# A Fourier mixer and a gated unit on one core: relayout of the first batch on VectorE, six chunks a batch on GpSimd, and new list offsets

## The chip, the cores and the metric

The kernel runs on one core of one Trainium2 chip. The metric is the device time of one execution in microseconds (us). The kernel before took 314.53 us in the median of three runs (318.61, 312.99, 314.53). The profiled execution, from which all rows in this document come, is a separate one and took 310.74 us, of which 309.0 us lie between its first and its last instruction.

## The reference

For each of 8 batches, `x` of 3200 positions and 256 channels goes through a real Fourier transform along the positions, is multiplied by a complex filter, and is transformed back. The result feeds a gated unit with a causal convolution over five positions for each channel:

```python
X = np.fft.rfft(x, axis=1)
Y = X * (filt_r + 1j * filt_i)[None, :, :]
y = np.fft.irfft(Y, n=3200, axis=1)
gate_pre[:, s] = sum(conv_w[k] * y[:, s + k - 4] for k in range(5))
out = ((1 / (1 + np.exp(-gate_pre))) * (y @ w_val)) @ w_out
```

## The kernel before

The transform of length 3200 is done as 100 x 32. All work is cut into tasks, each with a name of a stage, a batch and a number. The stages of batch `b`, in order of dependence:

- `li`, `lx`: GpSimd issues five loads for the batch (four of 96 partitions, one with the last four rows of all), which cast `x` to bf16 on the way into `xt`. The tile pool holds two batches.
- `s1` (L539): eight tasks of four matmuls with the table `cf_t`, each over a block of 32 channels and all four loads. `so` copies each result out of PSUM, `t` (L560) turns it on VectorE in 32 x 32 blocks into `tt`.
- `s2` (L570): seven chunks of frequencies (six of two, the last of one) with the table `w_t`.
- `xs`, `z` (L591): the product with the filter `f_t`. In batches 1 to 7 the chunks 1 to 5 are copied out of PSUM (`xs`) and multiplied on GpSimd; chunks 0 and 6 are multiplied by VectorE straight from PSUM. In batch 0 all seven are copied out and multiplied on VectorE.
- `ia` (L604): the first inverse step; `ue` copies out. Then the data changes layout through DRAM: `wr` (L624) writes a scratch tensor `escr`, and `lv` (L634, L635) reads it back as `vt`, once all seven writes of the batch have landed.
- `ib` (L644): the second inverse step, with the table `ci_t`; `ye` copies it out into `y_t`, one of two halves of the time signal's storage.
- `cv` (L665), `ga` (L676): the convolution with diagonal tiles `dg_t` in 32 x 32 blocks of TensorE, and the sigmoid on ScalarE. `cv` of a batch needs all eight `ye` of it. `vl` (L685) and `gv` (L696) make the gated value on TensorE and VectorE, `op` (L705) the output product, `oe` its copy out of PSUM, `store` the write.

Tasks of the kind "copy out of PSUM" (`so`, `xs`, `ue`, `ye`, `oe`) run on ScalarE or on VectorE; both helpers stand in one function, so that all of them appear as L264 (ScalarE) or L266 (VectorE). PSUM has four slots of 1024 words.

The order on every engine is fixed when the kernel is built. The class `Plan` holds a cost for each task, and at each step issues the ready task with the smallest rank. A rank is

```python
par["PERIOD"] * b + par["OFF"][s] + par["STEP"][s] * k + more
```

for stage `s`, batch `b` and number `k`; `more` comes from `HEAD` and differs from zero in batches 0, 1 and 7. `STAY` holds TensorE in one kind of matmul, `HOLD` and `UNTIL` keep copies from VectorE while ScalarE is about to be free. Costs and ranks only set the order of issue; on the chip each engine runs its list in order and waits where its operands are not there.

The filter is loaded by 24 transfers from GpSimd's queue (`fi`, L325 and L329), in two cuts: frequencies 0 to 5 (chunks 0 to 2) and 6 to 12 (chunks 3 to 6). Each cut is then doubled onto other partitions: the first by four transfers from SyncE's queue (`di`, L338), the second by four copies on VectorE (`dx`, L340). The first `z` needs the whole first cut. Transfers from GpSimd's queue run in the order of issue and share the 16 DMA engines with those of SyncE's queue.

Of the kernel before, what the change touches and what calls it, by code (L numbers as in the profile page):

```python
# [16 lines left out]
L = 100  # L17
R = 32
# [13 lines left out]
ZG = (1, 2, 3, 4, 5)  # L32
# [8 lines left out]
    PERIOD=69.33,  # L41
    STAY=17.41, HOLD=0.011, UNTIL=595.53,
    OFF=dict(ci=893.25, cv=136.43, dg=133.01, f=-99.31, ia=98.64, ib=140.46, lv=651.32, lx=112.25, op=334.8,
             pads=6.11, s1=79.04, s2=-92.81, tab=-546.84, vl=-14.07, wtn=485.78, wts=853.38, z=-353.3,
             zp=126.74),
    STEP=dict(ci=131.829, cv=29.199, dg=2.091, f=48.78, ia=21.353, ib=22.278, lv=131.77, lx=8.372, op=9.386,
             pads=12.629, s1=3.933, s2=18.8, tab=72.012, vl=60.741, wtn=92.585, wts=60.233, z=99.415,
             zp=53.742),
    HEAD={
        0: dict(ci=-528.2, cv=-3.9, dg=102.12, f=-304.44, ia=230.55, ib=-168.14, lv=-173.59, lx=172.89,  # L50
             op=-8.32, pads=454.98, s1=-170.57, s2=49.09, tab=-917.46, vl=2.17, wtn=-336.16, wts=-367.93,
             z=92.17, zp=106.55),
        1: dict(ci=183.19, cv=-50.24, dg=104.68, f=49.05, ia=-320.73, ib=-66.17, lv=65.54, lx=-361.7,
             op=0.84, pads=-248.75, s1=-427.17, s2=-23.57, tab=-126.37, vl=10.42, wtn=18.08, wts=-351.07,
             z=137.9, zp=68.79),
        2: dict(ci=79.61, cv=-396.79, dg=204.22, f=-51.32, ia=-236.72, ib=-480.77, lv=65.54, lx=294.66,
             op=-0.81, pads=-238.81, s1=18.19, s2=-77.31, tab=8.17, vl=496.8, wtn=143.78, wts=-454.11,
             z=324.38, zp=166.29),
# [152 lines left out]
def kernel(  # L211
# [20 lines left out]
    ci_t = cpool.tile([128, L], FP16, name="ci_t")  # L232
    w_t = cpool.tile([128, NS, 64], FP16, name="w_t")
# [7 lines left out]
    wn_t, wq_t = (y_t[0][...].rearrange("p h n -> p (h n)")[:, o:o + 2 * D]  # L241
                  .rearrange("p (h e) -> p h e", h=2) for o in (2 * NS * 64, 2 * NS * 64 + 2 * D))
# [10 lines left out]
    gpool = ctx.enter_context(tc.tile_pool(name="gate", bufs=NGB))  # L253
    opool = ctx.enter_context(tc.tile_pool(name="ost", bufs=NOB))

    V = nc.vector
    st, g = {}, {}

# [9 lines left out]
    def small(shape, dtype, name):  # L268

        words = math.prod(shape[1:]) * (1 if dtype == FP16 else 2) // 2  # L270
        o = g["small"] = g.get("small", NS * 64) + words
        assert o <= H + N, o
# [32 lines left out]
    def load_x(b, j):  # L305
        w = R // NX
        if j == 0:
            st["X", b] = xpool.tile([128, NX, XROW], BF16, name="xt")
# [53 lines left out]
    def pool_setup():  # L362
# [3 lines left out]
        for j in range(NX + 1):  # L366
            load_x(0, j)
# [38 lines left out]
    def w_dve():  # L406
# [28 lines left out]
        g["sg"] = sg  # L435
# [48 lines left out]

    def ci_dve():
# [11 lines left out]
        for o, t in zip((vm, vt, vh, vc), fields):  # L497
            V.tensor_copy(o[...], t[...])
        kv, ph, wt, mt = col("kv"), col("ph"), col("wt"), col("mt")
        V.tensor_scalar(ph[...], vc[...], 25.0, 25.0, op0=ALU.mult, op1=ALU.add)  # L500
        V.scalar_tensor_tensor(kv[...], vt[...], 13.0, vm[...], op0=ALU.mult, op1=ALU.add)
        V.scalar_tensor_tensor(kv[...], vh[...], 26.0, kv[...], op0=ALU.mult, op1=ALU.add)
        ix = small([128, L], FP32, name="ix")
        ts(vc[...], vc[...], 1.0, ALU.add)
        V.tensor_scalar(ix[...], g["af"][...], kv[:, 0:1], ph[:, 0:1], op0=ALU.mult,
                        op1=ALU.add)
        ts(mt[...], kv[...], 0.0, ALU.is_equal)
        ts(ix[...], ix[...], 0.01, ALU.mult)
        V.scalar_tensor_tensor(mt[...], kv[...], 50.0, mt[...], op0=ALU.is_equal, op1=ALU.add)
        V.tensor_scalar(wt[...], kv[...], 50.5, 2.0, op0=ALU.is_lt, op1=ALU.mult)  # L510
        g["fx"] = frac(ix, "x", [128, L])
        V.tensor_tensor(mt[...], mt[...], vc[...], op=ALU.mult)
        V.tensor_tensor(wt[...], wt[...], mt[...], op=ALU.subtract)
        ts(wt[...], wt[...], 1.0 / L, ALU.mult)
        g["wt"] = wt

    def ci_act():
        g["sx"] = small([128, L], FP32, name="sx")
        sine(g["sx"][...], g["fx"][...])

    def ci_mul():
        ts(ci_t[...], g["sx"][...], g["wt"][:, 0:1], ALU.mult)
# [23 lines left out]

    def so(b, q, e):
# [5 lines left out]
    def turn(b, q):  # L553
        if q == 0:
# [3 lines left out]
                    for v in (st.pop(("SO", b, q))[...],  # L558
# [37 lines left out]
    def inva(b, u):  # L596
# [3 lines left out]
        for a in range(nm):  # L600
            for w, tab in enumerate((a_t, b_t)):
                for t, h in ((0, 0), (1, 1), (0, 1), (1, 0)):
                    rows = slice(64 * t, 64 * t + 64)
                    nc.tensor.matmul(  # L604
                        ps[64 * h:64 * h + 64, 512 * t + D * a:512 * t + D * a + D],
# [5 lines left out]
    def ue(b, u, e):  # L611
        nm = UCH[u][1]
        ps = st.pop(("ia", b, u))
        t = st["U", b, u] = upool.tile([128, 2, 2, D], BF16, name="u")
# [3 lines left out]
    def wr(b, u):  # L618
        if ("E", b) not in st:
# [7 lines left out]
            in_=t[:, 0:nm].rearrange("p m t d -> p (m t) d"))  # L627

# [43 lines left out]
    def gate(b, j):  # L672
        n = 128 * BLK[j][1]
        ps = st.pop(("cv", b, j))
        t = st["G", b, j] = gpool.tile([128, 2, 512], BF16, name="gt")
# [15 lines left out]
    def gv(b, j):  # L691
        n = 128 * BLK[j][1]
        gt = st.pop(("G", b, j))
        ps = st.pop(("vl", b, j))
        t = st["GV", b, j] = gpool.tile([128, 2, 512], BF16, name="gv")
# [3 lines left out]
    def outp(b, j):  # L699
        nm = BLK[j][1]  # L700
        t = st.pop(("GV", b, j))[:, :, 0:128 * nm].rearrange("p h (n a) -> p h a n", a=nm)
# [7 lines left out]
    def oe(b, j, e):  # L709
        nm = BLK[j][1]  # L710
        ps = st.pop(("op", b, j))
        o = st["O", b, j] = opool.tile([128, 4 * D], FP32, name="o")
        copy(e, o[:, 0:nm * D], ps[:, 0:nm * D])

    def store(b, j):
        m0, nm = BLK[j]
        o = st.pop(("O", b, j))
# [5 lines left out]
    plan = Plan(dict(ring=43, ps=NPS, xt=NXT, so=NSO, t=2, xs=NXS, z=NZ, u=NU, e=2, v=NVB, y=2, g=NGB, gv=NGB,  # L723
# [16 lines left out]
    for b in range(B):  # L740
        for j in range(NX + 1):
# [6 lines left out]
            else:  # L748
                add(f"li0,{j}", {"none": 0.0}, 0, [], None, take=ring, lag=3.2 + 0.55 * j)
            add(f"lx{b},{j}", {"DQ0": 1.97 if j < NX else 0.4}, r, [f"li{b},{j}"], None,  # L750
                lag=SBUF0, packet=0.324, give=ring)
        for q in range(NQ):
            r = rank("s1", b, q)
            add(f"s1{b},{q}", {"PE": 0.456}, r, [f"lx{b},{j}" for j in range(NX + 1)]
# [7 lines left out]
        for u, (m0, nm) in enumerate(UCH):  # L762
            r = rank("s2", b, u)
            cut = [n for n, c in enumerate(FCUT) if m0 < c[1]][0]
            pool = b > 0 and u in ZG
# [5 lines left out]
            if near:  # L771
# [10 lines left out]
                lambda e, b=b, u=u: inva(b, u), take=("ps", "u"), give=("z",), mode=1)  # L782
            add(f"ue{b},{u}", two(512 * nm), r, [f"ia{b},{u}"],
                lambda e, b=b, u=u: ue(b, u, e), give=("ps",), slot=(f"ia{b},{u}", 0))
            add(f"wi{b},{u}", {"SP": 0.37}, r, [f"ue{b},{u}"] + ([f"wi{b},{u - 1}"] if u else []),
# [3 lines left out]
        for i, (r0, nr) in enumerate(ICH):  # L789
            r = rank("lv", b, i)  # L790
            add(f"vi{b},{i}", {"SP": 0.75}, r, [f"wd{b},{u}" for u in range(NU_)],
# [6 lines left out]
                lambda e, b=b, i=i: ib(b, i), take=("ps",) + (("y",) if i == 0 else ()),  # L798
                give=("v",) + (("e",) if i == NI - 1 else ()), mode=0)
            add(f"ye{b},{i}", two(200 * nr), r, [f"ib{b},{i}", "pads"] + (  # L800
                [f"te{len(TCH) - 1},1", "cim", "dg"] if b == 1 and i == 0 else
# [121 lines left out]
```

## Time and profile before

| What | Value |
|---|---|
| Median of three runs | 314.53 us |
| Profiled execution: time, span | 310.74 us, 309.0 us |
| Busy share of the span: TensorE, VectorE, ScalarE, GpSimd | 83%, 81%, 74%, 58% |
| Mean granted TensorE clock | 0.974 |
| DMA | 70.35 MB, mean 228 GB/s |
| Chain that ended last | TensorE 50%, DMA 20%, VectorE 16%, GpSimd 5% |

The profiled time is 1.74 us longer than its span, which lies before the first and behind the last instruction. The shares are means over stages that differ: at the start TensorE has little to do, later almost no gap. A busy matmul need not run at full clock. Rows of a group of instructions give line, engine, operation, tiles, shapes and count, then busy time and the mean ns of one, then the idle time ahead of them. Rows of windows give the stretch, its length, and each engine's busy time with its count of instructions, then the granted clock, the DMA share and GB/s.

### The profile page before, as it was taken

The page shows a single profiled execution, that of the slowest core. Times are in us where ns is not written, and L with a number is a line of the kernel's source. Part 1 is how long each engine was busy: PE and PEld are TensorE (multiplying, and loading weights), DVE is VectorE, ACT ScalarE, POOL GpSimd, SP SyncE. Part 2 cuts the span into 40 slices and gives each one's busy share as a digit, 9 for nine tenths or more (in the row PEclk, how much of TensorE's full clock was granted, in tenths as well). Part 3 has the DMA queues.
Part 4 walks back from the last instruction along what each step waited for, and adds up shares of the span by engine and source line. Part 5 has one row for each costly group of instructions (what it writes and reads, how often), then busy time and mean ns, then how long its engine had stood idle before and what let it go on. Part 6 is the DMA issues. An engine that isn't in the chain of part 4 may idle for free.

```text
span 309.0 us, 11427 instructions
## 1 busy us (share of the span) xinstructions
PE 258.0 (83%) x4932; PEld 174.3 (56%) x4932; DVE 250.5 (81%) x304; ACT 228.8 (74%) x260; POOL 179.3 (58%) x117
## 2 busy tenths in 40 slices
PE   0292499948978999987997999899999999999993
PEld 0151244435645765664765667665776765767662
DVE  6976599984997989997997999797998895686763
ACT  2382488965997889778888778777988886767653
POOL 8394402499899889869922995079803992000000
PEclk9999999965999999999999999999999999999998
DMA  7999995989749999799889988963697687584665
GB/s 109 185 128 228 206 201 134 201 208 237 178 126 199 311 255 303 239 211 311 208 270 216 346 286 221 318 223 131 212 330 260 220 283 237 210 282 161 240 258 223
DMA packets 53154, 70.35 MB, mean 228 GB/s; under 512 B 6256, under 2 KB 35568, under 8 KB 53104
## 3 DMA queue, kind: packets, MB, share of 16 engines
q1 hardware_dynamic: 46032, 54.55, 52.5%
q0 software_dynamic: 7072, 15.08, 29.5%
q8 instruction: 39, 0.64, 0.8%
q14 instruction: 11, 0.09, 0.1%
HBM read 43.78 MB, written 39.85 MB: 271 GB/s over the span
## 4 chain that ended last, share of the span: by engine, by line
PE 50%; DMA 20%; DVE 16%; POOL 5%; issue 4%; ACT 3%; DVEq 0%; SPq 0%; ACTq 0%; POOLq 0%
PE ps L705 11%; PE ps L665 10%; PE ps L685 10%; DMA xt<-in_x_dram 8%; PE ps L539 6%; PE ps L644 5%; PE ps L604 5%; DMA vt<-escr 5%; DVE z L591 4%; DMA out_dram<-o 4%; DMA escr<-u 3%; DVE y L266 2%; PE ps L570 2%; DVE xs L266 2%; DVE tt L560 2%
## 5 line engine op out<-in xcount | busy, mean ns | idle before, releaser
L591 POOL TENSOR_TENSOR z<-xs,f_t 128x2048 bf16<-128x2048 bf16 x35 | 142.2, 4079 | 45.7 <-ACT xs L264 33.5
L696 DVE TENSOR_TENSOR gv<-ps,gt 128x1024 bf16<-128x1024 f32 (+1 forms) x56 | 61.3, 1105 | 14.8 <-PE ps L685 11.1
L676 ACT ACTIVATE gt<-ps 128x1024 bf16<-128x1024 f32 (+1 forms) x56 | 49.7, 930 | 14.7 <-PE ps L665 13.6
L264 ACT ACTIVATE so<-ps 128x1024 bf16<-128x1024 f32 x51 | 51.6, 1024 | 9.7 <-PE ps L539 8.1
L685 PE MATMUL ps<-y,wv_t 128*128 128x512 bf16 (+1 forms) x224 | 52.1, 357 | 2.2 <-issue 0.8
L705 PE MATMUL ps<-wo_t,gv 128*128 128x256 bf16 x400 | 51.9, 273 | 1.1 <-DVE gv L696 0.6
L539 PE MATMUL ps<-xt,cf_t 100*128 100x256 bf16 x256 | 47.6, 326 | 3.9 <-DMA f_t<-in_filt_i_dram 1.3
L705 PEld LDWEIGHTS <-gv 128*128 128x128 bf16 x400 | 41.3, 110 | 6.3 <-issue 2.3
L560 DVE STREAM_TRANSPOSE tt<-so 128x512 f32<-128x512 f32 x64 | 44.0, 700 | 0.6 <-ACT so L264 0.3
L665 PE MATMUL ps<-y,dg_t 32*32 32x512 bf16 (+1 forms) x2240 | 40.9, 355 | 3.2 <-DVE y L266 2.0
L264 ACT ACTIVATE u<-ps 128x1024 bf16<-128x1024 f32 (+1 forms) x39 | 37.6, 968 | 7.5 <-PE ps L604 7.1
L264 ACT ACTIVATE o<-ps 128x1024 f32<-128x1024 f32 (+1 forms) x34 | 31.7, 943 | 10.5 <-PE ps L705 9.4
L644 PE MATMUL ps<-ci_t,vt 104*128 104x100 f16 x512 | 34.4, 212 | 6.0 <-DMA vt<-escr 4.3
L604 PE MATMUL ps<-z,a_t 64*64 64x256 bf16 x416 | 30.2, 304 | 9.9 <-DVE z L591 8.2
L264 ACT ACTIVATE xs<-ps 128x1024 bf16<-128x1024 f32 (+1 forms) x28 | 28.1, 1008 | 13.6 <-DVE z L591 7.5
L644 PEld LDWEIGHTS <-vt 104*128 104x128 bf16 x512 | 28.2, 100 | 16.6 <-DMA vt<-escr 7.2
L264 ACT ACTIVATE y<-ps 128x800 bf16<-128x800 f32 x35 | 29.3, 839 | 10.7 <-PE ps L644 9.7
L539 PEld LDWEIGHTS <-cf_t 100*128 100x128 f16 x256 | 26.5, 112 | 18.8 <-issue 9.4
L266 DVE CAST y<-ps 128x800 bf16<-128x800 f32 x29 | 28.4, 987 | 8.4 <-PE ps L644 6.2
L665 PEld LDWEIGHTS <-dg_t 32*32 32x32 bf16 x2240 | 25.8, 88 | 15.3 <-issue 8.7
L570 PE MATMUL ps<-tt,w_t 64*64 64x256 bf16 x416 | 25.0, 312 | 8.1 <-DVE tt L560 5.7
L685 PEld LDWEIGHTS <-wv_t 128*128 128x128 bf16 x224 | 19.6, 97 | 19.7 <-issue 7.5
(71 smaller groups left out, 249.1 us busy)
## 6 DMA issues: line engine op xcount, KB each, us to landing
out_dram<-o SPq DMA_DIRECT2D x32, 512.0 KB
xt<-in_x_dram POOLq DMA_DIRECT2D x32, 384.0 KB, 7.4
escr<-u SPq DMA_DIRECT2D x48, 256.0 KB
vt<-escr SPq DMA_DIRECT2D x64, 192.0 KB
out_dram<-o SPq DMA_DIRECT2D x24, 384.0 KB
escr<-u SPq DMA_DIRECT2D x8, 128.0 KB
vt<-escr SPq DMA_DIRECT2D x64, 16.0 KB
f_t<-f_t SPq DMA_DIRECT2D x4, 192.0 KB
```

What stands on the lines that cost most here:

```text
L264: nc.scalar.activation(dst, src, AF.Copy, **kw)
L266: V.tensor_copy(dst, src)
L539: nc.tensor.matmul(ps[:, w * CQ * j:w * CQ * j + w * CQ], lhsT=cf_t[0:L].rearrange("p h c i -> p (h c i)"), rhs=st["X", b][0:L, j, 0:w * D ...
L560: V.transpose(dst, src)
L591: eng.tensor_tensor(z[:, :, :, 0:nm * D], src.unsqueeze(1).to_broadcast((128, 2, 2, nm * D)), f_t[:, :, :, m0:m0 + nm, :].rearrange("p w h ...
L604: nc.tensor.matmul(ps[64 * h:64 * h + 64, 512 * t + D * a:512 * t + D * a + D], lhsT=tab[rows, h, m0 + a, :], rhs=z[rows, w, h, D * a:D * ...
L644: nc.tensor.matmul(ps[:, o:o + L], lhsT=v[0:NV, a, 128 * dh:128 * dh + 128], rhs=ci_t[0:NV, :], start=True, stop=True)
L665: nc.tensor.matmul(ps[j][o:o + 32, 512 * dh:512 * dh + 128 * nm], lhsT=dg_t[rows, dh, k, :], rhs=y[rows, dh, 128 * m0 + k:128 * m0 + k + 1 ...
L676: nc.scalar.activation(t[:, :, 0:n], ps[:, :].rearrange("p (h n) -> p h n", h=2)[:, :, 0:n], AF.Sigmoid)
L685: nc.tensor.matmul(ps[:, 512 * eh:512 * eh + 128 * nm], lhsT=wv_t[:, dh, KIND[j], eh, :], rhs=y[:, dh, H + 128 * m0:H + 128 * m0 + 128 * n ...
L696: V.tensor_tensor(t[:, :, 0:n], ps[:, :].rearrange("p (h n) -> p h n", h=2)[:, :, 0:n], gt[:, :, 0:n], op=ALU.mult)
L705: nc.tensor.matmul(ps[:, D * a:D * a + D], lhsT=t[:, eh, a, :], rhs=wo_t[:, KIND[j], eh, :], start=(eh == 0), stop=(eh == 1))
```

## The change

1. First transform by pieces (`s10`, `so0`): in batch 0 a task takes one load of `x` and half of the channels, two matmuls of 512 columns, so that it needs only that load and the load of the last rows, which is now issued first. The transposes `t0` need one task of each of the four loads.
2. Inverse relayout of batch 0: `ue0` copies into the output buffers (`u0_t`), eight transposes on VectorE (`turn0`, tasks `tv`) write the gate buffers (`v0_t`), and `ib0` multiplies from there, with a second table `cj_t` in the order of rows that the transposes leave. Batch 0 writes and reads no scratch tensor any more. GpSimd clears the unused rows (`pads0`).
3. Gate and output buffers become two fixed tiles, `gg_t` and `oo_t`, with places handed out by hand, so that batch 0 can use them earlier for other data.
4. Chunk 6 of batches 1 to 7 is copied out of PSUM and multiplied on GpSimd too, so that GpSimd has six chunks a batch.
5. Every batch has offsets of its own in `HEAD`, and all ranks are new, so that the issue order differs on every engine. The two halves of the time signal are reserved one by one (`y0`, `y1`).

```diff
-ZG = (1, 2, 3, 4, 5)
+ZG = [()] + [tuple(range(1, 7))] * 7
...
-    PERIOD=69.33,
-    STAY=17.41, HOLD=0.011, UNTIL=595.53,
+    PERIOD=403.75,
+    STAY=443.98, HOLD=0.705, UNTIL=67.21,
...
-    more = par["HEAD"].get((0, 1, 7).index(b), {}).get(s, 0.0) if b in (0, 1, 7) else 0.0
-    return par["PERIOD"] * b + par["OFF"][s] + par["STEP"][s] * k + more
+    return (par["PERIOD"] * b + par["OFF"][s] + par["STEP"][s] * k
+            + par["HEAD"].get(b, {}).get(s, 0.0))
...
+    gg_t = cpool.tile([128, 2 * NGB, 2, 512], BF16, name="gg_t")
+    oo_t = cpool.tile([128, NOB, 4 * D], FP32, name="oo_t")
+
+    u0_t = oo_t[...].rearrange("p k n -> p (k n)").bitcast(BF16).rearrange(
+        "p (g i e) -> p g i e", i=32, e=E)
+    s0_t = gg_t[...].rearrange("p k h n -> p (k h n)").rearrange("p (g r e) -> p g r e", r=R, e=E)
+    v0_t = gg_t[...].rearrange("p k h n -> p (k h n)").rearrange("p (r g e) -> p r g e", r=R, e=E)
...
-        for j in range(NX + 1):
+        for j in (NX, *range(NX)):
             load_x(0, j)
...
+    def cj_dve():
+        kv, keep = col("kj"), col("keep")
+        ts(keep[...], g["lo"][...], NS - 0.5, ALU.is_lt)
+        V.scalar_tensor_tensor(kv[...], g["hi"][...], 26.0, g["lo"][...], op0=ALU.mult, op1=ALU.add)
+        ci_turn(1, kv, g["cc"], keep)
...
+    def s10(k):
+        j, hh = k // 2, k % 2
+        ps = psum()
+        for a in range(2):
+            o = 128 * hh + 64 * a
+            nc.tensor.matmul(ps[:, 512 * a:512 * a + 512],
+                             lhsT=cf_t[0:L].rearrange("p h c i -> p (h c i)"),
+                             rhs=st["X", 0][0:L, j, 0:R // NX * D]
+                             .rearrange("p (r d) -> p r d", d=D)[:, :, o:o + 64]
+                             .rearrange("p r (g e) -> p g r e", e=E),
+                             start=True, stop=True)
+        st["s1", 0, k] = ps
...
+    def pads0():
+        nc.gpsimd.memset(u0_t[:, :, NS:32, :], 0.0)
+
+    def turn0(k):
+        src = u0_t[:, GQ * k:GQ * k + GQ].rearrange("p g i e -> p (g i e)").bitcast(FP32)
+        dst = v0_t.rearrange("p r g e -> p (r g e)").bitcast(FP32)
+        V.transpose(dst.rearrange("p (r g w) -> p g w r", r=R, w=E // 2)[:, GQ * k:GQ * k + GQ],
+                    src.rearrange("p (g i w) -> p g w i", i=32, w=E // 2))
+
+    def ib0(i):
+        dh, r0 = i // 4, 8 * (i % 4)
+        ps = psum()
+        for a in range(8):
+            o = 512 * (a // 4) + L * (a % 4)
+            nc.tensor.matmul(ps[:, o:o + L], lhsT=v0_t[:, r0 + a, 32 * dh:32 * dh + 32, :]
+                             .rearrange("p g e -> p (g e)"),
+                             rhs=cj_t[...], start=True, stop=True)
+        st["ib", 0, i] = ps
...
+                add(f"tv{i}", {"DVE": 0.70}, r, [f"ue0,{u}" for u in range(NU_)]
+                    + ([f"tv{i - 1}"] if i else []), lambda e, i=i: turn0(i))
+                r = rank("ib", 0, i)
+                add(f"ib0,{i}", {"PE": 0.37}, r, [f"tv{4 * (i // 4) + 3}", "cjm"]
+                    + ([f"ib0,{i - 1}"] if i else []), lambda e, i=i: ib0(i),
+                    take=("ps",) + (("y0",) if i == 0 else ()), mode=0)
...
-            pool = b > 0 and u in ZG
+            pool = u in ZG[b]
```

More of the change, by code (lines that the diff above doesn't have):

```diff
@@ L252 @@
     vpool = ctx.enter_context(tc.tile_pool(name="ivi", bufs=NVB))
-    gpool = ctx.enter_context(tc.tile_pool(name="gate", bufs=NGB))
-    opool = ctx.enter_context(tc.tile_pool(name="ost", bufs=NOB))
     V = nc.vector
     st, g = {}, {}
+    places = {"gt": list(range(NGB)), "gv": list(range(NGB, 2 * NGB)), "o": list(range(NOB))}
     def psum(n=0):
@@ L748 @@
             else:
[L749 removed]
+                add(f"li0,{j}", {"none": 0.0}, 0, [], None, take=ring,
+                    lag=3.2 + 0.55 * ((j + 1) % (NX + 1)))
             add(f"lx{b},{j}", {"DQ0": 1.97 if j < NX else 0.4}, r, [f"li{b},{j}"], None,
```

194 lines of the change are left out of this document (133 added, 61 removed).

## The prediction

> **What bounds the kernel now.** I read the windows first: busy time of TensorE, its weight loads, VectorE, ScalarE and GpSimd, then granted clock, DMA share and GB/s.
>
> ```profile
> span 309.0 us, 11427 instructions
> ...
> 34.17:61.09 26.92, 24.71 (x231) 13.08 (x231) 25.55 (x28) 23.11 (x28) 7.24 (x9) 1.00 0.93 183
> ...
> 87.09:304.70 217.61, 203.96 (x4340) 142.16 (x4340) 181.58 (x180) 172.74 (x193) 126.02 (x46) 1.00 0.80 246
> ...
> 90.00:100.00 10.00, 8.61 (x162) 5.34 (x161) 7.78 (x7) 8.76 (x10) 9.98 (x6) 1.00 0.88 180
> 130.00:140.00 10.00, 8.25 (x143) 5.32 (x124) 9.68 (x9) 8.08 (x9) 6.53 (x3) 1.00 0.97 235
> 140.00:150.00 10.00, 8.59 (x220) 5.79 (x224) 7.67 (x10) 7.64 (x10) 9.98 (x5) 1.00 1.01 287
> 160.00:170.00 10.00, 7.73 (x115) 5.53 (x114) 8.30 (x9) 8.30 (x9) 3.15 (x4) 1.00 1.02 239
> ```
>
> From the first convolution (87.09) to the last copy (304.7) TensorE is busy for 203.96 of 217.61 us: it is the bound there, with 13.65 us idle, half of it (1.39 + 1.75 + 1.41 + 2.27 = 6.8) in the four windows shown. Behind 304.7 come 4.3 us of copy and store. So a gain must come from an earlier first convolution or from the 13.65 us.
>
> The order in time, next, shows what places that convolution.
>
> ```profile
> 12.94 0.52 POOL L329 DMA_DIRECT2D f_t<-in_filt_r_dram  x1 [2.05 <-DMA xt<-in_x_dram]
> ...
> 18.54 8.88 SPq L338 DMA_DIRECT2D f_t<-f_t  x4
> ...
> 25.59 0.68 DVE L560 STREAM_TRANSPOSE tt<-so 128x512 f32<-128x512 f32 x1
> ...
> 34.17 2.36 DVE L591 TENSOR_TENSOR z<-xs,f_t 128x2048 bf16<-128x2048 bf16 x2 [4.32 <-DMA f_t<-in_filt_i_dram]
> ...
> 37.61 15.37 SPq L624 DMA_DIRECT2D escr<-u  x6
> ...
> 64.84 0.55 SPq L634 DMA_DIRECT2D vt<-escr  x1
> ...
> 69.67 0.85 PE L644 MATMUL ps<-ci_t,vt 104*128 104x100 f16 x8 [1.40 <-DMA vt<-escr]
> ...
> 87.09 1.35 PE L665 MATMUL ps<-y,dg_t 32*32 32x512 bf16 x80 [1.67 <-DVE y L266]
> ...
> 90.64 2.54 DVE L696 TENSOR_TENSOR gv<-ps,gt 128x1024 bf16<-128x1024 f32 x2 [0.51 <-PE ps L685]
> ```
>
> The first transposes end at 26.3, but the first product waits for the filter until 34.17. From there to 61 both VectorE (25.55 of 26.92) and TensorE (24.71) are nearly full. Then the data goes to DRAM and back; the first `ib` starts at 69.67.
>
> TensorE is full there for another reason.
>
> ```profile
> 56.53 1.04 PE L539 MATMUL ps<-xt,cf_t 100*128 100x256 bf16 x4
> ...
> 62.99 0.61 PE L539 MATMUL ps<-xt,cf_t 100*128 100x256 bf16 x4
> ...
> 73.05 1.01 PE L539 MATMUL ps<-xt,cf_t 100*128 100x256 bf16 x4 [0.44 <-DMA xt<-in_x_dram]
> ...
> 78.09 1.09 PE L539 MATMUL ps<-xt,cf_t 100*128 100x256 bf16 x8
> ...
> 61.09:64.50 3.41, 1.76 (x31) 1.17 (x30) 3.41 (x5) 3.10 (x7) 3.40 (x3) 1.00 0.71 150
> 64.50:78.16 13.66, 9.94 (x117) 6.44 (x117) 7.48 (x7) 7.23 (x8) 12.93 (x8) 0.50 1.00 234
> ```
>
> The same four matmuls take 1.01 where the granted clock is 0.50 and 0.61 where it is 1.00; at 56.53 they take 1.04. So although the windows before 61 show 1.00 (no clock record lies there), TensorE ran at half speed until 61.09, and again from 64.5 to 78.16.
>
> **The change, part by part.** Durations, from the groups by form:
>
> ```profile
> L560 DVE STREAM_TRANSPOSE tt<-so 128x512 f32<-128x512 f32 x64 | 44.0, 700 | 0.6 <-ACT so L264 0.3
> ...
> L591 DVE TENSOR_TENSOR z<-ps,f_t 128x2048 bf16<-128x2048 f32 x7 | 16.0, 2289 | 4.0 <-PE ps L570 4.0
> ...
> L591 DVE TENSOR_TENSOR z<-ps,f_t 128x1024 bf16<-128x1024 f32 x7 | 8.5, 1211 | 0.5 <-PE ps L570 0.5
> L591 DVE TENSOR_TENSOR z<-xs,f_t 128x2048 bf16<-128x2048 bf16 x6 | 7.1, 1203 | 4.4 <-DMA f_t<-in_filt_i_dram 4.3
> L340 DVE COPY f_t<-f_t 32x3584 bf16<-32x3584 bf16 x4 | 4.6, 1152 | 1.3 <-DMA f_t<-in_filt_r_dram 1.2
> L266 DVE CAST u<-ps 128x512 bf16<-128x512 f32 x3 | 2.0, 654 | 0.1
> ...
> L266 DVE CAST xs<-ps 128x1024 bf16<-128x1024 f32 x14 | 16.9, 1209 | 2.3 <-PE ps L570 2.2
> ...
> L266 DVE CAST y<-ps 128x800 bf16<-128x800 f32 x29 | 28.4, 987 | 8.4 <-PE ps L644 6.2
> ```
>
> *First transform by pieces: 0.* It can end the transposes some 4 us sooner, but VectorE waits for the filter behind them; the table `cj_t` (some 17 short VectorE instructions) goes into the same wait. Without that cover, both would count in full.
>
> *Filter later: +2.1.* In the new order of GpSimd's queue two pieces of batch 1 stand ahead of the last part of the first filter cut, where one did.
>
> ```profile
> 7.00:34.17 27.17, 10.92 (x108) 6.73 (x109) 19.06 (x53) 11.43 (x14) 15.56 (x32) 1.00 1.06 187
> ...
> xt<-in_x_dram POOLq DMA_DIRECT2D x32, 384.0 KB, 7.4
> ...
> L374 POOL MEMSET y<- 128x128 f32 x1 | 0.3, 264 | 0.0
> ```
>
> The DMA engines are full (1.06) at 187 GB/s, so 384 KB more take 2.1 us: first product at 36.3. The clearing of unused rows (1,536 words of two bytes a partition, by the memset row at most 12 x 0.26 = 3.2 us, at least half) stands ahead of filter loads too, where GpSimd waits for transfers anyway (2.05); bounds 0 and 3.2, I take 0, since the transfers in hand keep the DMA engines busy.
>
> *Relayout on VectorE.* It removes seven writes and sixteen reads of SyncE's queue (with their 15.37 us of issues from 37.61 on and the wait to 69.67) and adds eight transposes. No row shows one that writes with so wide a stride: below, the transpose row, 0.70; above, a copy from PSUM, 1.21; I take 0.70, the same instruction on the same size. VectorE's new list from the first product through the last `ye0`: six products at 1.20, a short one at 0.65, one from PSUM at 2.29, two filter copies at 1.15, fifteen `t` and eight `tv` at 0.70, five copies at 1.21, a short one 0.65, one `ye` 0.99: 36.2 us; neighbours overlap a little (two products took 2.36, not 2.41), so 35.5. Idle at the rate of 34 to 61 (1.4 in 26.9) adds 1.8. A new wait: the fifth transpose waits for the first two `ib0` on TensorE (0.85 each at half clock, one `t` of 0.70 between), 1.0, and the next two a little, 1.3 in all; behind them stand the last transpose and through it the second half of `ib0`. 36.3 + 35.5 + 1.8 + 1.3 = 74.9: first convolution at 75 instead of 87.1. In SyncE's queue batch 1's writes then stand behind the turns of the output weights alone and no longer among batch 0's reads; that costs nothing. At the upper bound of the transposes it would be 79.
>
> TensorE has to keep up: by its new list it has, from the first `ia` (37.6) to that convolution, 16 `s1` at 0.55 (eight matmuls 1.09), 8 `ib` at 0.43 (half of 0.85), nine and a half chunks of `s2` and ten and a half of `ia`:
>
> ```profile
> L570 PE MATMUL ps<-tt,w_t 64*64 64x256 bf16 x280 | 15.2, 279 | 2.3 <-issue 0.9 <-DVE z L591 0.7 <-DVE y L266 0.3
> ...
> 149.72 0.66 PE ps L604 x16
> ```
>
> that is 0.43 and 0.66 each, in all 23.2 us at full clock. With 92% busy (24.71 of 26.92) at half clock until 61.1, 10.8 are done; the rest takes 13.5 at full clock: 74.6. It just fits.
>
> *What moves behind the convolution.* Ahead of it stand 15 tasks fewer: seven `s1` (3.9), three chunks of `s2` and a short one (1.5), three of `ia` and a short one (2.3), 7.7 us. TensorE then has 203.96 + 7.7 = 211.6 left.
>
> *Chunk 6 on GpSimd: 0.* VectorE loses seven products of 1.21 and gains, with ScalarE, seven copies of about 0.65; GpSimd gets seven half products, below.
>
> *Lists.* The new ranks reorder everything behind 75; no row prices that. Bounds: none of the 13.65 us idle goes, or all 6.8 of the four windows. Three of them have the DMA engines at 0.97 to 1.02, and batch 0's scratch traffic, an eighth of it, is gone, so I credit half, 3.4; 10.25 stay.
>
> *Sum:* 75 + 211.6 + 10.25 + 4.3 = 301.2 span, with 1.74 around it 302.9 against 310.74, a ratio of 0.975. The median of the runs is 314.53, 1.2% above the profiled execution; on that scale, 306.6.
>
> **The rivals.**
>
> *Half clock to the end of the stage.* If TensorE is not released at 61, its 23.2 us take 46.4: convolution at 84, and with the idle time as before 84 + 211.6 + 13.65 + 4.3 = 313.6, on the runs' scale 319.2. For it: 64.5 to 78.16 fell back to half. Against: that followed waits for the relayout, which go. The Trainium skill ("TensorE: Matmul & The Clock Gate", Part 1: The HAM clock gate) says that about 3.4 us of sustained work release the clock and an idle window takes it back; by that this rival has no chance and the sum stays 306.6. The trace does not agree: 92% busy from 34 to 61 ran at half speed.
>
> *VectorE takes over.* Its first `gv` would stand 7.3 us behind `ye0` (three copies, a short one, a transpose, a product from PSUM), at 82.2. Behind 90.64 it now has 178.5 us of work (181.58 less 3.0 before it) and 35.6 idle; by the same durations the new list has 8 us more behind that point. With the idle time kept: 82.2 + 186.5 + 35.6 + 4.3 = 308.6, no gain, 314.1. Against: VectorE idles because TensorE is late.
>
> *GpSimd sets the end (slower).*
>
> ```profile
> L591 POOL TENSOR_TENSOR z<-xs,f_t 128x2048 bf16<-128x2048 bf16 x35 | 142.2, 4079 | 45.7 <-ACT xs L264 33.5
> ...
> 58.09:257.00 198.91, 153.23 (x57) 0.97 0.85 244
> ```
>
> Its products run from 58.1 to 257.0, with 45.7 us idle. Seven half products add 14.3. If the idle time stays, the last ends at 271.3; from there the kernel before needs 52.0 to its end, the new list has 5.2 us of matmuls fewer behind its last product: 318.1 span, 323.7. It decides once GpSimd's idle time stays above about 29 us (last product behind 254.4). For it: 33.5 of its idle time are waits for ScalarE's copies, and ScalarE gets more copies. Against: those copies waited for a place in a list that is now new, not for ScalarE's time.
>
> *The pieces do nothing:* already in the sum.
>
> **How the numbers follow.** Forecast 57%, its own range 300 to 312; half clock 12%; VectorE 16%; GpSimd 15%. About 2% is what a measurement of this kernel can tell from no change: of the forecast, 48 points lie below 308.2; GpSimd's case gives 13 to slower, the half clock 3, the rest is within. Low end: convolution at 73 and 6.8 idle make 295.7 span, 301.1, less the 0.5 to 1% by which runs differ, 298. High end: the half clock's 319; most of GpSimd's case is left out.
>
> **What would show it.** Right: first product near 36, no `escr` for batch 0, first convolution near 75, four `s1` matmuls of 0.61 from about 61 on, TensorE idle about 10 behind it. Wrong: a first product behind 39, matmuls of 1.0 behind 65, a convolution behind 80, or GpSimd's last product behind 255 with TensorE waiting on it.

## The result and the profile after

The changed kernel took 331.22 us in the median of four runs (329.52 to 334.88), the kernel before 315.24 us beside it; the ratio is 1.0514 with an interval of 1.042 to 1.0608. It is slower, where 306.6 us were forecast and 319 was the upper end. Runs of one kernel differ by up to 4%, so the ratios compare only the faster runs of each.

The profiled execution took 329.52 us, of which 327.8 are the span. First the windows of the changed kernel: the stretch from the first product to the first `ib0`, from there to the first convolution, and from there to the end of TensorE's last matmul, behind which, as behind the forecast's 304.7, only the last copy and its store stand (length, then busy time of TensorE, its weight loads, VectorE, ScalarE and GpSimd, then granted clock, DMA share, GB/s).

```profile
36.71:62.69 25.98, 19.38 (x229) 11.72 (x229) 25.42 (x29) 22.85 (x26) 6.38 (x6) 0.80 0.63 117
62.69:92.49 29.80, 11.38 (x145) 8.00 (x145) 14.98 (x14) 29.06 (x12) 15.04 (x8) 0.60 0.36 65
92.49:322.82 230.33, 211.77 (x4440) 147.22 (x4452) 190.05 (x192) 181.56 (x208) 149.41 (x56) 0.98 0.78 236
```

The first convolution starts at 92.49, not at 75. In the middle stretch TensorE is busy for 11.38 of 29.80 us and ScalarE for 29.06. Behind the convolution's start TensorE has 211.77 us of work and 230.33 - 211.77 = 18.56 us idle. So 92.49 + 211.77 + 18.56 + 5.0 make up the 327.8 us, where the prediction had 75 + 211.6 + 10.25 + 4.3. Two terms failed: the convolution by 17.5 us, the idle time by 8.3.

What ScalarE and VectorE do in the middle stretch, from the timeline (start, length, instruction, tiles, shapes, count, idle time before it), what TensorE waits for meanwhile, and last the same copies on ScalarE in the kernel before:

```profile
63.25 14.21 ACT L287 ACTIVATE y<-ps 128x800 bf16<-128x800 f32 x4
76.95 1.37 ACT L287 ACTIVATE u<-ps 128x1024 bf16<-128x1024 f32 x1
78.19 1.03 ACT L287 ACTIVATE so<-ps 128x1024 bf16<-128x1024 f32 x1
79.21 1.02 ACT L287 ACTIVATE xs<-ps 128x1024 bf16<-128x1024 f32 x1
80.77 10.67 ACT L287 ACTIVATE y<-ps 128x800 bf16<-128x800 f32 x3 [0.54 <-PE ps L710]
...
85.08 3.64 DVE L289 CAST y<-ps 128x800 bf16<-128x800 f32 x1 [2.64 <-PE ps L710]
...
67.00 0.82 PE L710 MATMUL ps<-cj_t,gg_t 128*128 128x100 f16 x8 [3.09 <-ACT y L287]
...
77.52 1.01 PE L577 MATMUL ps<-xt,cf_t 100*128 100x256 bf16 x4 [2.44 <-ACT y L287]
...
PE ps L710 <- ACT y L287: 7.5, 3, 3.1
PE ps L665 <- ACT y L287: 5.5, 2, 2.8
PE ps L628 <- ACT y L287: 3.0, 1, 3.0
PE ps L577 <- ACT y L287: 2.4, 1, 2.4
...
L264 ACT ACTIVATE y<-ps 128x800 bf16<-128x800 f32 x35 | 29.3, 839 | 10.7 <-PE ps L644 9.7 <-ACT xs L264 0.8
```

Four copies of `y` take 14.21 us, 3.55 each, and one on VectorE 3.64, where the same shape took 0.84 and 0.99 before. They are the copies of the first batch, `ye0`. Each holds its PSUM slot, so TensorE waits 18.4 us in all for a slot, in `ib0` and in other stages alike. The four matmuls of 1.01 at 77.52 are at half speed again, here behind waits (mean granted clock 0.60 in this stretch).

### The profile page after: what moved, and what is told of

It reads as the page before. It is cut to its first block, busy times and chain, and to the rows that moved or that the text cites. A ratio compares the mean times of both kernels' runs of the same rounds, so it can differ in the third digit from the quotient of the medians.

```text
span 327.8 us, 11338 instructions
## 1 busy us (share of the span) xinstructions
PE 253.2 (77%) x4900; PEld 171.1 (52%) x4916; DVE 253.3 (77%) x321; ACT 249.9 (76%) x268; POOL 196.1 (60%) x125
## 4 chain that ended last, share of the span: by engine, by line
PE 44%; DMA 23%; DVE 13%; ACT 12%; issue 3%; POOL 2%; SPq 0%; DVEq 0%; POOLq 0%; ACTq 0%
DMA vt<-escr 15%; PE ps L759 10%; PE ps L805 10%; PE ps L780 10%; ACT y L287 8%; DMA xt<-in_x_dram 6%; PE ps L665 4%; PE ps L577 4%; PE ps L738 4%; DMA f_t<-in_filt_r_dram 3%; PE ps L628 3%; DVE z L649 2%; DVE gg_t L794 2%; DVE tt L618 2%; ACT so L287 1%
## 5 line engine op out<-in xcount | busy, mean ns | idle before, releaser
L649 POOL TENSOR_TENSOR z<-xs,f_t 128x2048 bf16<-128x2048 bf16 (+1 forms) x42 | 156.6, 3758 | 38.9 <-ACT xs L287 19.1
L794 DVE TENSOR_TENSOR gg_t<-ps,gg_t 128x1024 bf16<-128x1024 f32 (+1 forms) x56 | 61.3, 1102 | 11.1 <-issue 3.9
L771 ACT ACTIVATE gg_t<-ps 128x1024 bf16<-128x1024 f32 (+1 forms) x56 | 49.9, 930 | 19.4 <-PE ps L759 19.4
L287 ACT ACTIVATE y<-ps 128x800 bf16<-128x800 f32 x40 | 52.0, 1378 | 7.4 <-PE ps L738 6.3
L805 PE MATMUL ps<-wo_t,gg_t 128*128 128x256 bf16 x400 | 51.9, 273 | 0.8 <-ACT xs L287 0.5
L665 PE MATMUL ps<-z,a_t 64*64 64x256 bf16 x416 | 30.0, 301 | 21.1 <-DVE z L649 14.1
L805 PEld LDWEIGHTS <-gg_t 128*128 128x128 bf16 x400 | 41.5, 110 | 6.5 <-issue 3.0
L287 ACT ACTIVATE oo_t<-ps 128x1024 f32<-128x1024 f32 (+2 forms) x36 | 33.9, 949 | 10.6 <-PE ps L805 8.3
L337 POOL DMA_DIRECT2D xt<-in_x_dram x32 | 17.0, 536 | 34.6 <-PE ps L577 33.1
L628 PE MATMUL ps<-tt,w_t 64*64 64x256 bf16 x416 | 24.9, 309 | 15.6 <-DVE tt L618 8.4
L289 DVE COPY oo_t<-ps 128x1024 f32<-128x1024 f32 (+1 forms) x24 | 26.2, 1091 | 8.1 <-PE ps L805 8.1
L289 DVE CAST u<-ps 128x1024 bf16<-128x1024 f32 (+1 forms) x24 | 27.2, 1143 | 3.5 <-PE ps L665 3.5
```

What stands on the lines that cost most here:

```text
L287: nc.scalar.activation(dst, src, AF.Copy, **kw)
L289: V.tensor_copy(dst, src)
L649: eng.tensor_tensor(z[:, :, :, 0:nm * D], src.unsqueeze(1).to_broadcast((128, 2, 2, nm * D)), f_t[:, :, :, m0:m0 + nm, :].rearrange("p w h ...
L665: nc.tensor.matmul(o, lhsT=tab[rows, h, m0 + a, :], rhs=z[rows, w, h, D * a:D * a + D], start=(w == 0), stop=(w == 1))
L771: nc.scalar.activation(t[:, :, 0:n], ps[:, :].rearrange("p (h n) -> p h n", h=2)[:, :, 0:n], AF.Sigmoid)
L794: V.tensor_tensor(t[:, :, 0:n], ps[:, :].rearrange("p (h n) -> p h n", h=2)[:, :, 0:n], gt[:, :, 0:n], op=ALU.mult)
```

## The experiments

**The copies of the first batch.** `ye0` reads PSUM in rows of `n` and writes `y` at steps of 32 elements, 64 bytes: each element of two bytes stands alone. The copies of the later batches write runs of four. The theory: the scattered write is the price. Rival: the order of reading.

*Runs of eight* (`e1_run8`):

```diff
-        dst = y_t[0][:, dh, H:H + N].rearrange("p (n r) -> p r n", r=R)[:, r0:r0 + 8]
-        copy(e, dst.rearrange("p (j r) n -> p j r n", j=2),
+        dst = y_t[0][:, dh, H:H + N].rearrange("p (n r) -> p n r", r=R)[:, :, r0:r0 + 8]
+        copy(e, dst.rearrange("p n (j r) -> p n j r", j=2),
...
-             .rearrange("p j (r n) -> p j r n", n=L))
+             .rearrange("p j (r n) -> p n j r", n=L))
```

> Change: the changed kernel with one edit: ye0 walks positions in the outer and r in the inner loop, so that it writes runs of eight bf16 (16 bytes) instead of single bf16 64 bytes apart. Same data, same lists. Theory (scattered write): each of the eight ye0 falls from 3.55 us on ScalarE and 3.64 on VectorE to about 0.85 and 1.0, the first convolution comes at 75 to 78 instead of 92.5, and the time falls by about the same 15 to 17 us, to 312 to 317 on the scale of the runs (ratio to before 0.99 to 1.01; 0.975 if the recorded forecast's other steps hold). Rival (lists): the copies get short, but the time stays above 322, because the new lists lose the time behind the convolution. Rival (read order): the copies stay near 3.5, since it is the order of reading PSUM that costs.

Measured: 316.91 us, ratio to before 1.0126 (1.0001 to 1.0252). The groups of the copies and the windows of this kernel:

```profile
L287 ACT ACTIVATE y<-ps 128x800 bf16<-128x800 f32 x40 | 32.8, 839 | 12.2 <-PE ps L738 8.7 <-PE ps L710 2.9
L289 DVE CAST y<-ps 128x800 bf16<-128x800 f32 x24 | 23.3, 981 | 6.0 <-PE ps L738 5.9
...
74.08 1.60 PE L759 MATMUL ps<-y,dg_t 32*32 32x512 bf16 x80
...
74.08:308.96 234.88, 213.68 (x4456) 147.00 (x4452) 191.44 (x193) 181.53 (x209) 154.08 (x59) 0.99 0.80 235
```

All copies are back at 0.84 and 0.98, and the convolution starts at 74.08, as forecast (75). This one edit takes 14.3 us off the median and 13.7 off the span of the profiled execution (327.8 to 314.1). The second failed term remains: 234.88 - 213.68 = 21.2 us idle up to the last matmul.

*A step of 16 bytes instead of 64* (`e2_stride16`), and the kernel *before with its first batch written one `r` after another* (`e3_before_scatter`):

```diff
-        dst = y_t[0][:, dh, H:H + N].rearrange("p (n r) -> p r n", r=R)[:, r0:r0 + 8]
+        o = H + 8 * L * (i % 4)
+        dst = y_t[0][:, dh, o:o + 8 * L].rearrange("p (n r) -> p r n", r=8)
```

```diff
+        if b == 0:
+            copy(e, dst[:, :, :, r0:r0 + nr].rearrange("p h n r -> p h r n"),
+                 src.rearrange("p h (r n) -> p h r n", n=L))
+            return
```

> Change: the changed kernel with ye0 still one r after another, single bf16 at a time, but written 16 bytes apart instead of 64 (into another order of batch 0's signal, so batch 0's output is not the reference's; all else is done). It tells whether the price goes by the element or by the distance. Theory (a price for each new 64-byte line): four writes share a line; if neighbours in one line are not merged because they follow each other, the copy takes between 0.9 and 1.8 us. Rival (by the element of two bytes, whatever the distance): 3.5 us as before. Rival (reading order): 3.5 us too, since the reads are unchanged.

> Change: the kernel before, with batch 0's eight ye written one r after another, single bf16 64 bytes apart, instead of runs of four. Theory (scattered write): these eight take 3.5 us instead of 0.84 and 0.99, some 21 us more work in ScalarE and VectorE around 70 to 87, and the first convolution is late by 8 to 20 us; the span goes from 309 to 317 to 328. Rival (the price comes with the new layout of PSUM or the new buffers): the copies stay below 1.1 and the span at 309.

Measured: 337.15 and 328.82 us, one run each. The timelines of ScalarE:

```profile
63.72 14.44 ACT L287 ACTIVATE y<-ps 128x800 bf16<-128x800 f32 x4
...
69.74 7.37 ACT L264 ACTIVATE y<-ps 128x800 bf16<-128x800 f32 x2
...
103.44 2.37 PE L669 MATMUL ps<-y,dg_t 32*32 32x512 bf16 x80 [3.74 <-DVE y L266]
```

A step of 16 bytes costs the same (3.61 each). In the old layout, with the old buffers and lists, the scattered write alone costs 3.69 a copy (7.37 for two) and moves the convolution from 87.09 to 103.44. Reading in rows of `n` is not the cause: `xs` and `so` read PSUM from end to end too, and 1024 elements take 1.02. The copies at steps of 4 bytes, next, settle it: they read the same rows in the same order and take 1.03.

*Runs of two* (`e8_run2`), *steps of 4 and of 8 bytes* (`e22_stride4`, `e23_stride8`):

```diff
+        for c in range(2):
+            copy(e, dst.rearrange("p n (j r) -> p j n r", j=2)[:, :, :, 2 * c:2 * c + 2],
+                 ps[:, :].rearrange("p (j n) -> p j n", j=2)[:, :, 0:4 * L]
+                 .rearrange("p j (r n) -> p j n r", n=L)[:, :, :, 2 * c:2 * c + 2])
```

```diff
+        c, o = i % 2, H + 16 * L * (i % 4 // 2)
+        dst = y_t[0][:, dh, o:o + 16 * L].rearrange("p (n c) -> p c n", c=2)[:, c]
```

```diff
+        dst = y_t[0][:, dh, H:H + N].rearrange("p (n c) -> p c n", c=4)[:, i % 4]
```

> The kernel with runs of eight, but each copy of the first batch's y is split into two copies of 128x400 elements that write runs of two bf16 (4 bytes) each. Theory 'a price for each separate run written': 200 runs at the 4.4 ns that an isolated element cost (3.55 us by 800), 0.9 to 1.0 us for a copy. Rival 'only an element of two bytes by itself is dear, four bytes go at the full rate': 0.5 us (0.18 + 400 x 0.00083). Rival 'a price for each element once runs are under eight bytes': 1.8 us.

> The changed kernel, with each copy of the first batch's y writing its 800 elements of two bytes with a step of 4 bytes (the output of batch 0 is in another order). Theory 'an element of two bytes that no neighbour joins to four bytes is dear wherever it lies': 3.5 us a copy, as at steps of 64 and 16 bytes, and 327 to 338. Rival, the Trainium skill's rule (SBUF - State Buffer, under the engine doors' ports: lines of 16 bytes, at least two accesses for each line needed for the full rate): four elements of a copy fall on one line here, so 0.84 us a copy, and about 317.

> The changed kernel, with each copy of the first batch's y writing its elements with a step of 8 bytes (the output of batch 0 is in another order). Theory of the lone element: 3.5 us a copy. Rival, the rule of lines of 16 bytes: two elements for each line, just enough, 0.84 us a copy.

Measured: 318.49, 316.69 and 322.59 us, one run each. The copies on ScalarE:

```profile
L287 ACT ACTIVATE y<-ps 128x400 bf16<-128x400 f32 x14 | 6.1, 513 | 2.9 <-PE ps L710 2.9
...
63.59 3.08 ACT L287 ACTIVATE y<-ps 128x800 bf16<-128x800 f32 x3
...
64.35 7.39 ACT L287 ACTIVATE y<-ps 128x800 bf16<-128x800 f32 x4
```

800 elements one by one take 1.03 us at steps of 4 bytes, 1.85 at 8, 3.61 at 16 and 3.55 at 64; 400 in runs of two, 64 bytes apart, take 0.51, the full rate (on the line through 0.84 for 800 and 1.02 for 1024). So both ideas behind the steps of 4 and 8 bytes, that every lone element is dear and that two elements on a line of 16 bytes are enough, fall in part. A lone element is not dear at a step of 4. The Trainium skill ("SBUF — State Buffer", Specifications) speaks of lines of 16 bytes that need at least two hits for full bandwidth. The doubling up to 16 bytes, with no more beyond, agrees with such a line. At steps of 4, 8 and 16 bytes a copy enters 200, 400 and 800 such lines, so each further line costs 4.1 to 4.4 ns; this estimate holds for lone elements only, since the run of two enters 200 lines in 0.51. That two hits suffice holds here for a run of two, not for two elements 8 bytes apart (1.85 against 0.84).

**The idle time behind the first convolution.** With the copies mended the lead of the first batch is lost later. From the traces, the start of the first sigmoid of each batch (us):

| batch | 0 | 1 | 2 | 3 | 4 | 5 | 6 | 7 |
|---|---|---|---|---|---|---|---|---|
| before | 88.4 | 120.7 | 158.0 | 186.7 | 212.8 | 245.8 | 268.6 | 286.3 |
| runs of eight | 77.0 | 116.7 | 152.1 | 176.0 | 214.0 | 248.0 | 271.5 | 292.6 |

The lead is gone between the first sigmoids of batches 3 and 4. TensorE's waits behind the first convolution, before and with runs of eight (total, times, longest):

```profile
PE ps L644 <- DMA vt<-escr: 2.7, 4, 1.0
PE ps L665 <- DVE y L266: 2.0, 2, 1.7
PE ps L570 <- issue: 0.9, 1, 0.9
```

```profile
PE ps L738 <- DMA vt<-escr: 7.2, 6, 2.3
PE ps L759 <- issue: 3.6, 4, 1.5
PE ps L759 <- ACT gg_t L771: 1.4, 1, 1.4
```

The longest of its waits is for the relayout's loads of the later batches, 7.2 of the 21.2 us. Four explanations were tried: the sixth chunk on GpSimd, the order in SyncE's queue, DMA traffic, and the copies of ScalarE and VectorE.

*Chunk 6* (`e4_run8_zg5`, `e10_run8_z6dve`, `e14_before_z6pool`). The first goes back to five chunks and lets the planner order the work anew; the second keeps the order and computes the product on VectorE; the third gives chunk 6 to GpSimd in the kernel before.

```diff
-ZG = [()] + [tuple(range(1, 7))] * 7
+ZG = [()] + [tuple(range(1, 6))] * 7
```

```diff
-            add(f"z{b},{u}", {"POOL": 0.17 + 1.95 * nm} if pool else
+            add(f"z{b},{u}", {"POOL": 0.17 + 1.95 * nm} if pool and u < 6 else
```

```diff
+            if u == 6:
+                x6 = x6pool.tile([128, 2, D], BF16, name="x6")
+                V.tensor_copy(x6[...], src)
+                eng, src = nc.gpsimd, x6[...]
```

> Change: as the run with runs of eight, and chunk 6 of batches 1 to 7 back on VectorE straight from PSUM (five chunks on GpSimd); the planner orders the rest with the same ranks. Theory (chunk 6 costs nothing, as the prediction had it): within 1% of the run with runs of eight. Rival (GpSimd is short): faster by 2 to 4%, with the last product of GpSimd earlier by some 14 us. Rival (VectorE is short): slower by 1 to 3%.

> The kernel with runs of eight and the order of all its work written out as it is, except that the product of chunk 6 of the batches 1 to 7 is done by VectorE at that place (0.6 us each from the copy that is there already) instead of GpSimd (2.13 us). Theory G, the sixth chunk on GpSimd makes each batch late and that is where the idle time of TensorE behind the first convolution comes from: GpSimd's last product of batch 7 about 265 instead of 267.7, idle time down from 22 us to 15, time 309 to 312 against 316.9. Theory O, it is the order in the queues: idle time as before, 315 to 319.

> The kernel before with one edit: chunk 6 of the batches 1 to 7 is copied from PSUM by VectorE (0.65 us, where its product from PSUM took 1.2 us) and multiplied by GpSimd (2.1 us); all lists as they were. Theory G, the sixth chunk on GpSimd is what costs: 320 to 324 (7 times 2 us less what is covered), TensorE waits on GpSimd. Rival, GpSimd has room (it was idle for about a third of the time behind 87 us): within 1% of the kernel before.

Measured: 331.01 us (ratio 1.0603, 1.0451 to 1.0755), 321.2 us (1.0239, 1.0116 to 1.0362) and 319.76 us (1.0211, 1.0117 to 1.0305). The window behind the first convolution of the second, and TensorE's longest wait there in the third:

```profile
74.41:314.08 239.67, 212.75 (x4440) 148.03 (x4452) 194.48 (x200) 182.29 (x209) 138.86 (x51) 0.99 0.77 230
...
PE ps L609 <- POOL z L596: 5.7, 4, 2.3
```

In the new order GpSimd's sixth chunk is not what costs: with that product on VectorE TensorE idles 26.9 us instead of 21.2, and the ratio is no lower (1.0239 against 1.0126, the intervals overlap). In the old order the sixth chunk does cost some 2%, and the waits on GpSimd point at how. Order and share of the work were made for each other; the first of the three, where the planner answers with another order, tells of that order and not of the chunk.

*Loads ahead of stores* (`e11_run8_loads4`): only this stretch of SyncE's list is changed (`si` a store, `vi` a load of the relayout, with batch and number).

```diff
-si2,4 vi4,0 vi4,1 si3,0 vi4,2 vi4,3
+vi4,0 vi4,1 vi4,2 vi4,3 si2,4 si3,0
```

> The kernel with runs of eight and the order of all its work written out as it is, except that on the SP queue the first four loads of batch 4's relayout stand ahead of two stores (batch 2 and 3); a store there waited 10.9 us for a copy by ScalarE, and the loads were issued at 185.4 though the writes they need had been issued by 173.9. Theory O, loads held behind stores in the SP queue make the idle time: loads near 176, the last product ahead of batch 4's convolution 4 to 9 us earlier, TensorE's idle time in 175 to 225 us down from 6.0 to 2 or 3, time 312 to 314. Rival, this wait is covered, since TensorE had other work in it (busy 21.3 of 25 us): 316 to 318, and the chain of waits shows another piece in its place.

Measured: 315.85 us over ten runs, ratio 1.0004 (0.9919 to 1.0088): not to be told from 1.0126 (1.0001 to 1.0252). SyncE's queue in the profiled execution:

```profile
174.15 4.48 SPq L902 DMA_DIRECT2D out_dram<-oo_t  x2
178.73 1.52 SPq L771 DMA_DIRECT2D escr<-u  x1
184.58 0.33 SPq L808 DMA_DIRECT2D vt<-escr  x1
```

The loads still left at 184.58 (185.38 with runs of eight): the last write that they need, at 178.73, stood behind two other stores. The wait moved by one place; this experiment decides nothing.

*The first batch free of its relayout, in the old order* (`e15_before_free0`):

```diff
     def wr(b, u):
+        if b == 0:
+            st.pop(("U", b, u))
+            return
...
     def lv(b, i):
+        if b == 0:
+            return
...
-        v = st.pop(("V", b, i))
+        v = st.pop(("V", b, i)) if b else f_t[:, 0, 0]
```

> The kernel before, with the writes and loads of the first batch's relayout left out and its inverse matmuls fed from a tile of the filter that is long there, so that the first batch waits for no DMA; all lists and everything else as they were (the output of batch 0 isn't the reference's). It asks what an early first convolution is worth with no other part of the change. Theory V, little of it arrives at the end, because the later batches' products and relayouts do not come earlier with it (at 100 us the kernel with runs of eight had 190.4 us of TensorE's work left against 192.8 before, for a first convolution 13 us earlier): first convolution at 76 to 80, the last one within 3 us of before, time 311 to 315 on the runs' median of 316. Rival W, an early first convolution is worth all its advance and the new lists lost it again: 304 to 308.

Measured: 311.97 us, ratio 0.9888 (0.9832 to 0.9944).

```profile
68.53 0.85 PE L649 MATMUL ps<-ci_t,f_t 104*128 104x100 f16 x8
...
87.53 0.84 PE L670 MATMUL ps<-y,dg_t 32*32 32x512 bf16 x39 [1.67 <-DVE y L266]
```

Both theories assumed that the convolution would move. It did not: 87.53 against 87.09, the first `ib` at 68.53 against 69.67, now with no wait before it (in an execution of 316.39 us). So the trip through DRAM did not place the first convolution of the kernel before; the order of the lists did, which puts `ib` and `ye` of batch 0 among the work of batches 1 and 2. What an early convolution is worth by itself stays untested; that the 1% comes from the traffic left out is argued, not shown.

*Less store traffic* (`e16_before_halfstore`, `e17_run8_halfstore`; an eighth in `e18_run8_fewstores`, `e19_before_fewstores`) and *shorter copies too* (`e20_run8_fewcopies`, `e21_before_fewcopies`). The edit for an eighth is shown; for a half the `8` is a `2`, and the second cut is in the last two only:

```diff
-        nc.sync.dma_start(out=dst, in_=o[:, 0:nm * D])
+        nc.sync.dma_start(out=dst[:, 0:nm * D // 8], in_=o[:, 0:nm * D // 8])
...
-        copy(e, o[:, 0:nm * D], ps[:, 0:nm * D])
+        copy(e, o[:, 0:nm * D // 8], ps[:, 0:nm * D // 8])
```

> The kernel before, each store writing only the first half of its columns (half of the output is left unwritten); all orders as they were. Theory D, the DMA engines hold up the loads of the relayout: waits for vt behind the first convolution are 2.7 us there, so at most 1 to 3 us come out, 313 to 315. Rival, DMA traffic is not what the loads wait for: 315 to 317.

> The kernel with runs of eight, each store writing only the first half of its columns; all orders as they were. Theory D: TensorE's waits for vt behind the first convolution fall from 7.2 us to below 3.5, and the time by 5 to 8 us more than half stores take off the kernel before: 308 to 311. Rival, the loads are late because the products and copies ahead of them are late, not because of the traffic: within 2 us of 316.9, waits for vt still 6 or more.

> The kernel with runs of eight, each store writing only the first eighth of its columns (the rest of the output is left unwritten). With half of the store traffic gone its profiled execution came down from 314.1 to 304.4 us and TensorE's idle time behind the first convolution from 22.1 to 16.3, while the kernel before came from 309.0 to 307.2. Theory D, the traffic delays the loads of the relayout, and this kernel suffers from it more than before: idle time 12 to 14 us, time 303 to 308, ratio to the kernel with an eighth of the stores of before below 0.99. Rival, the half-store execution was a lucky one: 311 to 315, the same gain as the kernel before has.

> The kernel before, each store writing only the first eighth of its columns (the rest of the output is left unwritten). Theory D: idle time behind the first convolution stays at 12 to 14 us, time 308 to 311 (half of the stores gave 311.2). Rival: it gains what the kernel with runs of eight gains.

> As the kernel with runs of eight and an eighth of the stores, and the copies of the product with the output weights take only the first eighth of their columns too, so that ScalarE and VectorE have some 40 us of copies less between them (the output is incomplete). Theory C, the copies of ScalarE and VectorE are what the loads wait behind: a further 5 us or more, and more than the kernel before gets from it. Rival, the two engines have room (81% and 77% busy behind the first convolution): within 2 us of the kernel with an eighth of the stores.

> As the kernel before with an eighth of the stores, and the copies of the product with the output weights take only the first eighth of their columns too. Theory C: gains less from it than the kernel with runs of eight does. Rival: the same gain, or none, within 2 us.

Measured, the median and the ratio to the kernel before, run beside it:

| | order before | runs of eight |
|---|---|---|
| all stores | 316.36 | 316.91, 1.0126 (1.0001 to 1.0252) |
| half | 311.19, 0.9898 (0.979 to 1.0006) | 313.73, no interval |
| an eighth | 309.22, 0.9852 (0.9743 to 0.9961) | 307.19, 0.9754 (0.9664 to 0.9844) |
| an eighth, short copies | 307.93, 0.9885 (0.9833 to 0.9937) | 304.12, 0.9739 (0.966 to 0.9819) |

Windows from the first convolution to the last matmul: runs of eight with half and with an eighth of the stores, then before with half and with an eighth (the last from an execution of 311.79 us); and the waits for `vt` of the first two.

```profile
73.32:300.67 227.35, 211.03 (x4456) 146.82 (x4452) 190.80 (x193) 181.49 (x208) 152.85 (x58) 0.99 0.68 188
...
74.82:300.40 225.58, 210.16 (x4440) 146.83 (x4452) 190.28 (x193) 181.80 (x209) 153.65 (x58) 0.99 0.58 148
...
86.20:303.31 217.11, 202.98 (x4340) 142.61 (x4340) 181.50 (x180) 172.62 (x193) 126.07 (x46) 1.00 0.68 189
...
88.79:306.57 217.78, 204.74 (x4323) 143.93 (x4340) 181.50 (x180) 172.43 (x193) 126.10 (x46) 0.98 0.57 145
```

```profile
PE ps L738 <- DMA vt<-escr: 4.3, 6, 1.3
...
PE ps L738 <- DMA vt<-escr: 2.4, 4, 1.5
```

With less traffic the new order's idle time falls from 21.2 to 16.3 and 15.4, its waits for `vt` from 7.2 to 4.3 and 2.4; the old order's idle time stays at 14.1 and 13.0 (13.65 before). One execution stands for each, but `e22_stride4` and `e8_run2`, with all stores and copies nearly as short, have 22.5 and 24.9 idle: the fall of 4.9 and 5.8 is more than the 3.7 between these three. In the runs an eighth of the stores takes 3.7 points off the new order and 1.5 off the old one, though the intervals of these two differences overlap a little. So DMA traffic is the largest part that could be shown, some 5 to 6 us. The shorter copies change little in either order (their intervals overlap with those of the line above). Why the new order suffers more is argued, not shown: in batches 1 to 7, from the last `ue` of a batch to its first `ye` before passed 9.7 to 18.6 us (mean 15.1), and with runs of eight four of the seven had 9.8 to 11.4, so that a late load is felt at once; the other three had 14.3, 14.7 and 26.9.

## Why the prediction was wrong, by its steps

- *The copies `ye0`* are the step that failed most. They were priced by rows of copies that write runs of four elements (one `ye` at 0.99 in VectorE's list, the rest on ScalarE unpriced). The sum bounded the transposes' wide stride, but not the copies', which the same change made. They cost 3.55 and 3.64, and the convolution came 17.5 us late; the one edit that mends them takes off 13.7 us of the span.
- *The idle time behind the convolution*: "I credit half, 3.4; 10.25 stay". It rose to 18.6, and to 21.2 with the copies mended. The credit's reason, an eighth less scratch traffic, left out what the new order itself could add to the waits. Of the 11 us that this term missed, 5 to 6 go with the store traffic; the rest is open.
- *The premise* that the relayout places the first convolution: its loads out of the way, the old order kept it at 87.5. The convolution at 74.08 came with the new lists; whether they would have reached it through DRAM too was not tried.
- *Transposes*: 0.70 taken, bounds to 1.21. Measured:

```profile
L702 DVE STREAM_TRANSPOSE gg_t<-oo_t 128x512 f32<-128x512 f32 x8 | 8.3, 1057 | 5.7 <-PE ps L710 5.5
...
36.71 1.23 DVE L649 TENSOR_TENSOR z<-xs,f_t 128x2048 bf16<-128x2048 bf16 x1 [2.73 <-DMA xt<-in_x_dram]
...
L697 POOL MEMSET oo_t<- 128x1536 bf16 x1 | 1.4, 1397 | 0.0
```

  1.06, nearer the upper bound, 2.9 us more for eight. The convolution still met 75 once the copies were mended, partly by luck: with runs of eight VectorE was busy for 35.87 of the 38.07 us from its first product (36.01) to the convolution, so its list did set the time, as forecast, but the rest of the list was some 2.5 us shorter than priced, and it idled 2.2 for 3.1.
- *First product* at 36.71 for 36.3: right; the clearing took 1.40, and the first product came only 0.4 late. *Work moved behind*: 211.77 for 211.6 (213.68 with runs of eight), right.
- *Chunk 6 at 0*: GpSimd's last product ended at 281.7, behind the 254.4 of that rival, but TensorE has no wait on GpSimd among its largest, and moving the product back gained nothing. No cost was seen in this order, 2% in the old one.
- *Half clock*: the sign, matmuls of 1.01 behind 65, is there, but TensorE worked 11.38 of 29.80 us in that stretch; it was late for the slots. The sum for TensorE, half speed until 61 and full speed behind it, did not come true either. With runs of eight the same four matmuls took:

```profile
52.16 0.60 PE L577 MATMUL ps<-xt,cf_t 100*128 100x256 bf16 x4 [0.20 <-ACT oo_t L287]
...
56.23 1.03 PE L577 MATMUL ps<-xt,cf_t 100*128 100x256 bf16 x4
...
67.59 1.03 PE L577 MATMUL ps<-xt,cf_t 100*128 100x256 bf16 x4
...
70.88 0.60 PE L577 MATMUL ps<-xt,cf_t 100*128 100x256 bf16 x4 [0.23 <-DVE so L289]
```

  TensorE ran at full speed at 52, at half at 56 and still at 67, and the convolution came at 74.08 all the same, since TensorE was busy for only 27.09 of the 38.07 us. That "it just fits" was luck. Nor is half speed until 61 a property of the old list: with the same list in `e15_before_free0` four of these matmuls took 0.60 at 44.21. *VectorE takes over*: no, it is busy 190.05 of 230.33 us.

## What to carry to other kernels

Price a copy by where its elements land, not by its shape: for each access pattern that a change turns round, look for a row with the same run length and step, and without one give the bounds. Before crediting a removed wait with the time it ended, ask whether the list would have let the work start sooner. A denser order is not only the sum of its work: what had slack before (here the loads of the relayout) sets the pace when traffic delays it.

## What the hardware showed that was not expected

A copy of 800 two-byte elements out of PSUM took 0.84 us in runs, 1.03 at steps of 4 bytes, 1.85 at 8, and 3.55 to 3.69 from 16 bytes on, on ScalarE; VectorE took 1.06 at 4, 1.97 at 8, 3.71 at 16 and 3.64 at 64, against 0.98. Two neighbours written together, 64 bytes from the next two, were enough for the full rate (400 elements in 0.51). A 32 x 32 transpose that writes with a wide stride took 1.06 instead of 0.70.
